# A Fourier-mixing and feed-forward kernel: another written order for some 400 pieces of preparation, and SyncE held to it

## The chip, the cores and the metric

The kernel runs on one core of a Trainium2 chip. The time is the device time of one execution in microseconds (us), lower being better. A core has five engines with queues of their own: TensorE (PE, matrix products; PEld is its loading of weights), VectorE (DVE), ScalarE (ACT), GpSimdE (POOL) and SyncE (SP). An engine works through its own instructions strictly in the order in which the program hands them over; engines wait for one another through semaphores. SP does no arithmetic here: its queue issues transfers between DRAM and on-chip memory, and POOL's queue issues others. A transfer is issued when its queue reaches it and the semaphores it needs have come.

## The reference

```python
h  = x + A(layernorm(x))     # A: a = n @ hid_re.T, b = n @ hid_im.T, y = seq_re @ a - seq_im @ b
h2 = h + B(layernorm(h))     # B: silu(h @ w1) @ w2
```

Here x has 2048 rows of 512 values (f32), the two sequence matrices have 2048 x 2048 values, the two hidden matrices 512 x 512, w1 has 512 x 1792 and w2 1792 x 512. The layer norms have no weights.

## The kernel before

**Products.** Each f32 matrix is split into a rounded part `hi` and a remainder `lo` (`rounded`, L195 on ACT for `hi`, L199 or L201 on DVE for `lo`), and a product is three matrix products, hi by hi, hi by lo and lo by hi (`three`, L245, L246, L247). Much of the arithmetic is in Strassen-like forms: seven products of sums of blocks instead of eight products of blocks, with the sums made by DVE (L647 for the blocks of the sequence matrices), by POOL's accumulating loads (L662), or in the accumulators.

**Stages.** Real part then imaginary part of the sequence matrix on the even rows (`plain`, `fast`), mixing with the hidden matrices (`mix(0)`), the same for the odd rows (`fast` twice and `mix_fast(1)`), then for each half of the rows the layer norm (`norm_h`, with POOL's sum over partitions at L914), the up-projection (`up`), SiLU, and the down-projection (`down`).

**A written order.** The function `program` doesn't run anything itself. It collects about 1500 numbered events. Each has a planned time, and a function that emits a few instructions. `step` adds a block of matrix products at the running planned time of TensorE (0.2265 us for each product) and, at given leads before it, its preparation: loads, roundings, remainders and sums; what reads the accumulators stands at given delays after it. At the end the events are sorted by planned time plus a correction from the table `MOVED`, which names events by their number. `fnet_ffn_kernel` then emits event after event. For the engines in the tuple `ORDERED`, every instruction is tied behind the previous one of the same engine (`issue_after`), so that the engine's queue has exactly the written order. SP isn't in the tuple before: for its transfers the framework's scheduler chooses an order within what data and buffers allow.

**Buffers.** On-chip memory is cut into 51 pages. `Plan.places` hands pages to tiles in the written order, taking the page that is free earliest by plan. So a changed order also changes which page a tile gets, and so whose last use a load has to wait for.

**Names used further on.** `raw` is a 512 KB piece of a sequence matrix as loaded (`load_seq`, L371; the three blocks of a Strassen set by `load`, also L371), `ph` and `pl` are its rounded part and its remainder, `h` is a piece of x for the residual (`load_h`, L737 and L733), `hr`, `m`, `v`, `rs`, `tk` belong to the layer norm, `wal` is the remainder of an up weight, `Ul` and `Vl` are remainders of down weights, `g` is the hidden activation (L1067 to L1073), `vx` an accumulator of the up-projection. The event numbers used below are: 434 to 436, load, rounding and remainder of the imaginary part's block `raw01100`; 439, 443, 447 and 451, the loads of the four blocks `raw01211`, `raw01311`, `raw01011`, `raw01111`; 389 and 391, load of the residual piece `h01` and the sum into it; 475, a sum of blocks with its load 478; 562 and 563, rounding and remainder of `raw11100` for the product 564; 602, a sum of blocks of the last set, with its load 605; 416 and 417, DVE's Newton steps for the layer norm and, at the end of 417, POOL's store `tk`; 657, POOL's accumulating load of `raw11011` for the product 658; 748, the row mean `m10`; 800 and 802, `Ul` and `Vl` of one pair of weights; 890, a `wal`; 861 and 873, additions into `g`; 879 and 882, products of the up-projection.

Of the kernel before, what the change touches and what calls it, by code (L numbers as in the profile page):

```python
# [41 lines left out]
KEEP_US = 2, 0  # L42
FREE_US = {None: 2.0, "matmul": 4.0, "dma_start": 10.0}
MOVED = {
# [42 lines left out]
}  # L87
ORDERED = (mybir.EngineType.PE, mybir.EngineType.DVE, mybir.EngineType.Activation, mybir.EngineType.Pool)


class Stub:
# [44 lines left out]
def fnet_ffn_kernel(  # L136
# [29 lines left out]
    for *_, f in events:  # L166
# [5 lines left out]
        for ins in traced[n:]:  # L172
            if ins.engine in ORDERED:
                last[ins.engine] = ins
# [1199 lines left out]
```

## Time and profile before

| | |
|---|---|
| median of 3 runs | 694.58 us (693.73 to 699.06) |
| profiled execution | 695.98 us, span 694.2 us |
| mean granted TensorE clock | 0.989 |
| PE busy | 674.1 us, 97% of the span, 2916 matrix products |
| DVE busy | 569.2 us, 82% |
| ACT busy | 363.3 us, 52% |
| POOL busy | 99.5 us, 14% |
| transfers | 189.59 MB, mean 273 GB/s |

The span is what the profiler saw between first and last instruction; the time of the same execution is 1.78 us longer. The views quoted in the prediction are these: the page's first line (span), its part 1 (busy time of each engine), part 4 (what the chain that ended last is made of) and parts 5 and 6 (groups of instructions and of transfers); a table by stretches of the span, whose columns are the stretch, its length, then busy time and number of instructions of PE, PEld, DVE, ACT and POOL, the granted clock, the busy share of the 16 DMA engines and GB/s; the list of waits, with total, number and longest in us; and the chain that ended last, in order of time, as start, length and what it was.

### The profile page before, as it was taken

Reading aid. Unit: us, or ns where it says so; the run is one execution under the profiler, and the core shown is the slowest. Engines: PE = TensorE matmul, PEld = TensorE weight load, DVE = VectorE, ACT = ScalarE, POOL = GpSimd, SP = SyncE. Lnnn points to the kernel's source line nnn. Section 1 sums busy time; section 2 is a strip of 40 time slices with the busy share of each in tenths; the row PEclk is TensorE's granted clock in tenths of the full one; section 3 lists DMA queues with packets and bytes.
Section 4 is the critical chain, followed back from the end, with each engine's and each line's share of the span. In section 5 each row is a group of like instructions: output and inputs, shape, how many; then the busy total and the mean of one; then the engine's idle time right before and its main releaser. Section 6 shows DMA issues by size and latency. Waiting matters only on the chain.

```text
span 694.2 us, 8329 instructions
## 1 busy us (share of the span) xinstructions
PE 674.1 (97%) x2916; PEld 550.6 (79%) x2916; DVE 569.2 (82%) x723; ACT 363.3 (52%) x459; POOL 99.5 (14%) x130
## 2 busy tenths in 40 slices
PE   9999999999998899979998998999999999999997
PEld 6888888878886688868886886888888888888886
DVE  7999999898676898789998999766999556549884
ACT  6898656643533443536434654656755444557420
POOL 0011201111221232021411004241100000000000
PEclk9999999999999999999999999999999999999999
DMA  8949989968799976898889998746997496577802
GB/s 317 399 133 286 318 311 334 271 160 320 266 335 397 320 225 152 272 370 292 268 267 306 418 359 291 286 142 193 390 410 304 130 327 228 190 261 249 297 37 92
DMA packets 61786, 189.59 MB, mean 273 GB/s; under 512 B 6960, under 2 KB 14640, under 8 KB 61744
## 3 DMA queue, kind: packets, MB, share of 16 engines
q1 hardware_dynamic: 46608, 136.33, 55.6%
q0 software_dynamic: 14848, 52.46, 23.5%
q8 instruction: 23, 0.38, 0.2%
q10 hardware_dynamic: 288, 0.26, 0.1%
q14 instruction: 19, 0.16, 0.1%
HBM read 142.88 MB, written 46.15 MB: 272 GB/s over the span
## 4 chain that ended last, share of the span: by engine, by line
PE 82%; DVE 7%; DMA 4%; issue 4%; POOL 2%; ACT 1%; DVEq 0%; POOLq 0%; SPq 0%; ACTq 0%
PE m L246 8%; PE m L247 8%; PE m L245 7%; PE y L245 7%; PE y L246 7%; PE y L247 7%; PE f L245 6%; PE f L247 6%; PE f L246 6%; DMA raw<-in_seq 4%; PE c L247 3%; PE c L245 3%; PE c L246 3%; PE vx L245 3%; PE vx L246 3%
## 5 line engine op out<-in xcount | busy, mean ns | idle before, releaser
L195 ACT ACTIVATE ph<-raw 128x1024 fp32r<-128x1024 f32 x102 | 104.7, 1054 | 119.4 <-DMA raw<-in_seq 43.6
L199 DVE TENSOR_TENSOR pl<-raw,ph 128x1024 fp32r<-128x1024 f32 x92 | 110.5, 1219 | 19.4 <-ACT ph L195 18.8
L246 PE MATMUL m<-pl,S 128*128 128x512 f32 x192 | 75.2, 392 | 1.6 <-DVE pl L199 1.6
L245 PE MATMUL m<-ph,S 128*128 128x512 f32 x192 | 75.2, 391 | 0.5 <-ACT ph L195 0.5
L247 PE MATMUL m<-ph,S 128*128 128x512 f32 x192 | 74.7, 389 | 0.0
L1073 DVE TENSOR_TENSOR g<-vx,g 128x512 f32<-128x512 f32 x42 | 28.8, 689 | 48.1 <-PE vx L247 21.4
L246 PE MATMUL m<-pl,X 128*128 128x512 f32 x144 | 58.4, 406 | 6.9 <-DVE pl L199 6.9
L245 PE MATMUL f<-gth,wf 128*128 128x512 f32 x161 | 62.6, 389 | 0.0
L247 PE MATMUL f<-gth,wf 128*128 128x512 f32 x161 | 62.6, 389 | 0.0
L246 PE MATMUL f<-gtl,wf 128*128 128x512 f32 x161 | 62.6, 389 | 0.0
L245 PE MATMUL m<-ph,X 128*128 128x512 f32 x144 | 57.9, 402 | 2.9 <-ACT ph L195 2.9
L195 ACT ACTIVATE gth<-g 128x1024 fp32r<-128x1024 f32 x42 | 42.8, 1052 | 32.2 <-DVE g L1190 29.1
L247 PE MATMUL m<-ph,X 128*128 128x512 f32 x144 | 58.0, 403 | 0.0
L647 DVE TENSOR_TENSOR raw<-raw,raw 128x1024 f32<-128x1024 f32 x36 | 46.6, 1294 | 9.1 <-DMA raw<-in_seq 8.8
L199 DVE TENSOR_TENSOR gtl<-g,gth 128x1024 fp32r<-128x1024 f32 x42 | 50.6, 1215 | 2.9 <-ACT gth L195 2.8
L246 PEld LDWEIGHTS m<-pl,S 128*128 128x128 f32 x192 | 36.3, 189 | 10.7 <-DVE pl L199 3.1
L245 PEld LDWEIGHTS m<-ph,S 128*128 128x128 f32 x192 | 36.3, 189 | 8.5 <-ACT ph L195 0.9
L247 PEld LDWEIGHTS m<-ph,S 128*128 128x128 f32 x192 | 36.1, 188 | 7.3
L246 PEld LDWEIGHTS m<-pl,X 128*128 128x128 f32 x144 | 28.0, 194 | 14.7 <-DVE pl L199 8.8
L1070 ACT ACTIVATE g<-y 128x512 f32<-128x512 f32 x42 | 24.9, 596 | 26.8 <-PE y L247 26.0
L245 PEld LDWEIGHTS m<-ph,X 128*128 128x128 f32 x144 | 27.9, 194 | 9.6 <-ACT ph L195 3.7
L247 PEld LDWEIGHTS f<-gth,wf 128*128 128x128 f32 x161 | 30.2, 188 | 6.3
(334 smaller groups left out, 1588.0 us busy)
## 6 DMA issues: line engine op xcount, KB each, us to landing
raw<-in_seq SPq DMA_DIRECT2D x84, 512.0 KB, 6.9
wf<-wd SPq DMA_DIRECT2D x56, 512.0 KB, 6.2
sf<-sd SPq DMA_DIRECT2D x28, 512.0 KB, 4.9
raw<-in_seq POOLq DMA_DIRECT2D x16, 512.0 KB, 6.4
w<-in_ffn SPq DMA_DIRECT2D x28, 256.0 KB, 4.8
hf<-fd SPq DMA_DIRECT2D x12, 512.0 KB, 7.4
c<-cd SPq DMA_DIRECT2D x8, 512.0 KB, 5.7
h<-in_xT SPq DMA_DIRECT2D x8, 512.0 KB, 9.2
```

The costliest lines, as they stand in the source:

```text
L195: nc.scalar.activation(hi, src, AF.Copy, scale=sign)
L199: nc.vector.tensor_tensor(lo, src, hi, op=ALU.subtract)
L245: nc.tensor.matmul(acc, wh, mh, start=first, stop=False, skip_group_check=on)
L246: nc.tensor.matmul(acc, wh, ml, start=False, stop=False, skip_group_check=on)
L247: nc.tensor.matmul(acc, wl, mh, start=False, stop=last, skip_group_check=on)
L647: nc.vector.tensor_tensor(o, a, b, op=ALU.subtract)
L1070: nc.scalar.activation(g[q, f][:, tau, :], src, AF.Copy)
L1073: nc.vector.tensor_tensor(g[q, f][:, tau, :], src, g[q, f][:, tau, :], op=ALU.add)
```

## The change

Two things change. The table `MOVED` gets other entries, some 400 in each version, so that many loads, roundings, remainders, sums and stores stand earlier or later in the written order. TensorE's blocks stay in the same order. And SP joins `ORDERED`, so its transfers are issued in the written order as well. No instruction is added or removed on any engine: PE has 2916 matrix products, ACT 459 instructions, SP 305 transfers in both.

```diff
 MOVED = {
-    0: -36.389, 1: -26.974, 2: -25.939, 4: -11.243, 5: -2.693, 6: -13.747, 12: 14.791, 14: 14.711, 16: 18.149,
...
-    382: -6.701, 385: -6.084, 386: 12.11, 389: -8.794, 392: 29.565, 393: 10.825, 394: -2.4, 395: -5.773, 396: -8.195,
-    399: 0.585, 407: 9.82, 413: 3.675, 416: 9.909, 417: 10.994, 418: 18.286, 419: 14.954, 420: 19.968, 421: 22.38,
-    426: -13.409, 427: -12.306, 428: -9.978, 431: -5.315, 434: -7.091, 435: -8.466, 448: 5.682, 449: 6.113,
-    457: 5.344, 458: 6.173, 466: 3.109, 470: 3.472, 472: 4.448, 473: 2.565, 474: 3.664, 475: 4.827, 476: 3.713,
...
-    562: 7.247, 563: 6.96, 566: -21.988, 567: -8.316, 568: -8.975, 571: -7.565, 572: -2.707, 583: -10.317,
-    584: -9.857, 585: -10.429, 591: -8.989, 600: -9.323, 602: -14.47, 603: -9.883, 604: -9.605, 605: -13.05,
...
-    652: -17.791, 655: 6.183, 656: 6.402, 657: 8.938, 660: 3.784, 666: 3.041, 667: 5.105, 668: 2.916, 669: 9.103,
...
-    743: -16.636, 744: -15.219, 747: 8.561, 748: 5.353, 749: 1.425, 750: 8.476, 751: 5.341, 752: 5.487, 753: 5.039,
...
-    791: -29.354, 793: 21.242, 796: 17.891, 797: 18.541, 798: 15.638, 799: 30.528, 800: 30.551, 801: 22.376,
-    802: 28.878, 803: 30.882, 804: -37.203, 805: -35.339, 806: -22.187, 807: -16.326, 810: 6.765, 811: -11.914,
...
-    849: 10.95, 850: -35.58, 851: -12.549, 852: -12.388, 853: -12.17, 861: 6.54, 862: 5.955, 864: 2.581, 865: 5.264,
-    871: 1.743, 873: 2.177, 874: 4.867, 876: 2.03, 881: 14.176, 890: 0.614, 922: -0.032, 923: -1.532, 1040: 3.011,
...
+    0: -28.65, 28: 5.71, 32: 7.37, 35: 4.85, 36: 5.08, 38: 5.92, 39: 3.77, 40: 11.88, 41: 4.45, 42: 5.82, 46: 6.79,
...
+    371: -2.93, 379: 15.77, 380: -5.83, 381: -9.58, 382: -11.55, 383: -10.71, 385: -12.74, 389: 15.56, 392: 31.21,
...
+    413: 2.52, 416: 2.35, 419: 4.93, 421: 4.41, 422: -5.38, 423: -11.72, 424: -12.78, 427: 1.2, 434: -20.43,
+    435: 8.14, 436: 7.8, 441: 6.79, 444: 6.24, 445: 7.12, 448: 6.88, 449: 4.71, 456: 6.48, 457: 6.32, 458: 4.15,
+    469: 3.35, 470: 4.72, 475: -7.82, 478: -8.29, 480: -9.25, 481: -3.04, 486: 5.35, 487: 3.91, 490: 6.07, 493: 3.56,
...
+    551: -22.18, 562: -1.92, 566: -13.21, 567: -7.28, 572: 4.19, 575: 2.87, 576: 4.05, 578: 8.24, 579: 2.78,
+    580: 2.84, 582: 12.19, 583: -11.4, 584: -6.49, 585: -8.06, 591: -11.48, 597: 5.63, 600: -8.75, 602: -6.54,
+    603: -5.42, 604: -6.58, 605: -7.77, 615: -5.2, 616: -5.83, 618: -10.76, 628: 5.64, 632: -4.62, 635: -9.76,
...
+    739: 5.09, 740: -12.75, 741: -12.8, 743: -5.88, 748: 10.99, 749: 12.27, 750: 14.31, 751: 14.39, 752: 15.61,
...
+    793: 19.36, 794: -6.35, 795: -1.97, 796: 16.67, 797: -43.41, 799: 25.35, 800: 23.26, 801: 12.21, 802: 23.15,
...
 }
-ORDERED = (mybir.EngineType.PE, mybir.EngineType.DVE, mybir.EngineType.Activation, mybir.EngineType.Pool)
+ORDERED = (
+    mybir.EngineType.PE, mybir.EngineType.DVE, mybir.EngineType.Activation, mybir.EngineType.Pool, mybir.EngineType.SP,
+)
```

Of the events named above, 436 and 478 have no entry before; 417, 563, 657, 861, 873 and 890 have none after.

63 rows, old and new, of the table MOVED are left out of this document.

## The prediction

> **What bounds the kernel now.** I read the page's first parts first, to see which engine could set the time.
>
> ```profile
> span 694.2 us, 8329 instructions
> PE 674.1 (97%) x2916; PEld 550.6 (79%) x2916; DVE 569.2 (82%) x723; ACT 363.3 (52%) x459; POOL 99.5 (14%) x130
> PE 82%; DVE 7%; DMA 4%; issue 4%; POOL 2%; ACT 1%; DVEq 0%; POOLq 0%; SPq 0%; ACTq 0%
> ```
>
> TensorE is busy for 97% and makes 82% of the chain that ended last; the rest of the chain is what TensorE waited for. No matrix product is taken away, so the change can only win or lose waits. Next, where they lie: the table by stretches, PE busy being its second number.
>
> ```profile
> 216.00:244.00 28.00, 23.31 (x92) 17.62 (x91) 21.37 (x22) 11.69 (x14) 4.95 (x3) 0.94 0.95 341
> 300.00:314.00 14.00, 9.95 (x37) 7.71 (x36) 11.17 (x9) 4.18 (x6) 4.93 (x3) 0.88 0.94 369
> 360.00:376.00 16.00, 13.73 (x53) 10.62 (x52) 12.49 (x16) 6.87 (x8) 2.01 (x3) 0.89 0.94 265
> 428.00:442.00 14.00, 11.23 (x43) 8.78 (x43) 13.36 (x15) 6.48 (x11) 8.17 (x8) 0.88 0.79 296
> 437.50:690.00 252.50, 252.47 (x1113) 208.47 (x1111) 185.18 (x245) 129.15 (x179) 16.33 (x20) 1.00 0.68 240
> 26.00:100.00 74.00, 73.98 (x327) 60.95 (x326) 71.42 (x110) 55.48 (x73) 11.34 (x17) 1.00 0.88 284
> ```
>
> In the undisturbed 252.50 us one product takes 252.50/1113 = 0.227 us. The four short stretches need (92-1), (37-1), (53-1) and (43-1) times 0.227, one product being cut by a border; they lose 7.3, 5.8, 4.2 and 4.5 us, together **21.8 us**. Part of each loss is not waiting but a granted clock of 0.88 to 0.94. Everything else is nearly full: after 437 TensorE loses 0.03. So the least that a better order could give is about 695.98 - 21.8 = 674 for the profiled execution.
>
> What ended these waits is in the chain, in order of time.
>
> ```profile
> 214.93 8.05 DMA raw<-in_seq
> 223.06 1.07 ACT ph L195
> ...
> 225.29 1.22 DVE pl L199
> ...
> 236.44 1.24 DVE pl L199
> 237.72 0.50 PE m L246
> 239.15 0.42 PE m L245
> 239.56 0.43 PE m L246
> ...
> 294.37 9.36 DMA raw<-in_seq
> 303.91 1.05 issue
> 304.96 1.23 DVE pl L199
> 306.23 0.50 PE m L246
> ...
> 313.66 1.22 DVE pl L199
> 314.88 1.14 DVE raw L647
> ...
> 356.24 0.53 POOL tk L955
> 356.77 8.62 DMA raw<-in_seq
> 365.47 1.06 ACT ph L195
> 366.56 1.24 DVE pl L199
> 367.84 0.50 PE m L246
> ...
> 421.59 1.13 DVE Ul L199
> ...
> 430.37 1.14 DVE m L912
> 431.57 0.57 issue
> 432.14 1.29 DVE g L1073 x2
> 433.48 0.72 PE vx L245
> ```
>
> Three waits begin with a transfer of a sequence block (`raw<-in_seq`), the fourth with DVE's own queue.
>
> **The change part by part.** All counts stay, so no duration is added; each part moves what an engine does next.
>
> First wait, 216 to 244 (7.3 us). Events 439, 443 and 447 are written well ahead of 214.93, but before the change SP's order has 451 in front of them, whose page was held by a store from `hS10l`.
>
> ```profile
> SPq L371 <- DMA fd<-hS10l: 8.3, 1, 8.3
> h<-in_xT SPq DMA_DIRECT2D x8, 512.0 KB, 9.2
> ```
>
> In the written order 439 and 443 stand ahead of 451 and are spared up to those 8.3 us. What is late next: the remainder 436 now stands behind the sum 391, whose load 389 moves behind 443. That load needs the page of an earlier `pl`, about 207 by DVE's new order, and lands 9.2 later, 216; then 1.2 for the sum, 1.07 and 1.22 for the pair `ph`, `pl` (whose page is free only after another store, about 218): TensorE, which wants it at 218, waits some 2.4. The sum 475 now stands in front of two remainders on DVE and waits for its load 478, about 217 plus 8: another 2.3. I keep 5.3 of the 7.3 with what the clock adds, so **2.0 goes**; bounds 7.3 and -3 (475's load later by its own 2 to 3 us).
>
> Here the Trainium skill bears on what a leftover costs. After 237.72 the products start 0.43 apart, half speed, for some 3.4 us, 1.7 lost. "TensorE: Matmul & The Clock Gate", part 1, says the clock is cut by an activity window of about 3.4 us; split waits would then cost no half-speed spell, and 2.0 would become 3.7. The half speed here followed several waits in one stretch, so the row doesn't decide, and the sum goes without it.
>
> Second wait, 300 to 314 (5.8). DVE stood at the sum 602 for the load issued at 294.37 and landed at 303.73, while the `pl` for product 564 stood behind it. Now 563 stands ahead of 602 and seven other pieces, so this wait goes. What is late next: DVE's remainders for the following products, which already make up the chain again from 313.66 (`pl`, then `raw`). I keep half: **3.0 goes**, bounds 0 and 5.8.
>
> Third wait, 360 to 376 (4.2). On POOL's queue the accumulating load 657 stands behind the store `tk`, which waited for DVE's Newton steps till 356.24. They are moved ahead of some five pieces of 1.1 to 1.2 us, about 7 us earlier; load, `ph` and `pl` then end near 361, and the product wants them at 363.6. **4.2 goes**; bounds 0 and 4.2.
>
> Fourth wait, 428 to 442 (4.5). Here DVE is late by its own work.
>
> ```profile
> 372.00:430.00 58.00, 58.00 (x257) 48.06 (x256) 55.66 (x53) 29.99 (x33) 9.94 (x13) 1.00 0.93 349
> DVE raw L647 <- DMA raw<-in_seq: 4.1, 2, 2.7
> DVE pl L199 <- ACT ph L195: 4.5, 3, 3.5
> ```
>
> It works 55.66 of 58 us, so whatever TensorE gains earlier, it arrives here and finds DVE no further. Ahead of product 882 (2.7 us of TensorE behind 879) DVE's new queue holds two weight remainders of 1.13 more (`Ul`, `Vl`) and the mean's two pieces less, from 430.37 to the additions at 432.14, 1.8: some 0.5 net. So DVE allows 882 earlier by 2.7 - 0.5 = **2.2 plus what DVE itself is earlier**. DVE is earlier where it stood in the same waits as TensorE: 2.0 in the first and 3.0 in the second (it waited 4.1 and 4.5 there and behind for loads and roundings), 5.0 together; bounds 0 and 8.6 + 2.0. In the third it did other work. So the gain at 437 is 5.0 + 2.2 = **7.2**, although TensorE alone would have 2.0 + 3.0 + 4.2 = 9.2 by then.
>
> The start, 26 to 100. DVE works 71.42 of 74 us, and sums and weight pieces are pulled forward into it; up to some 2 us of remainders come late at 80 to 130. SP's order also puts two loads behind five others; their `ph` are moved later too, so nothing stands for them. Near 283 a remainder stands behind three other DVE pieces of about 1.2 and may be 2.7 late. I count all of these at nothing, because DVE's work up to 437 is the sum and a wait of TensorE in between is cover that it had anyway; if DVE isn't late at 433, they cost up to 4.7.
>
> After 437 DVE has 67 us to spare, and TensorE waits nowhere; some 100 stores and loads move there. Nothing, with a bound of 5.8 for one wait like the second.
>
> Sum: 695.98 - 7.2 = 688.8 for the profiled execution, which is 1.40 above the median of the runs; against the median 694.58 - 7.2 = 687.4. I predict **687**.
>
> **The rivals.**
>
> *All four waits go.* If DVE's standing for loads (8.6 in the second half, 2.0 and more in the first) goes too, 16 to 21 us are won: 674 to 679. For it: all three causes upstream are reordered. Against it: DVE's 55.66 of 58 us. Chance 0.20.
>
> *The waits only move.* DVE gains nothing upstream, and one new wait near 283 (2.7) and one after 437 eat the 2.2: 690 to 698. For it: 436 and 475 are put behind late loads. Chance 0.12.
>
> *The loads land no earlier.* The DMA engines are busy 0.94 to 0.95 of the first and second wait; a load issued 8 us earlier then shares the engines with those that went before, and lands as it did. The first wait's 2.0 and DVE's part of the second, 3.0, are gone: 694.58 - 2.2 = 692.4. The Trainium skill, "DMA: Bandwidth & Descriptors", section "Issuing engines are not separate DMA queues", says that transfers run on the same 16 engines whoever issues them, and that issuing only saves time on the sequencer; by that rule this would be the time. Against it: outside the waits the share is 0.68 to 0.93, so there is room. Chance 0.06.
>
> *SyncE blocks (the slower side).* Held to an order, SP stands at a load whose page isn't free, and every load behind it stands too, also those whose page is free.
>
> ```profile
> SPq L371 <- PE m L247: 47.5, 14, 13.4
> raw<-in_seq SPq DMA_DIRECT2D x84, 512.0 KB, 6.9
> ```
>
> Before, SP could stand 13.4 us without harm, since the scheduler put loads that nobody needed behind it. A stand of 13.4 ahead of a load with 6.9 to land takes 20.3, against the 18 us by which loads are written ahead: 2.3 late, and 1.7 for the half clock, 4.0 each. It decides from the third such place on, beyond the 7.2 won: five of them are 20.0 - 7.2, 707. The places would be 185 to 225, where h loads are now in the row, and 385 to 410. Chance 0.18.
>
> *The change doesn't do what it says:* the pages held, not the order, set when SP issues, and the table's shifts cancel. Then 694.6. Chance 0.02.
>
> **How the numbers follow.** The forecast has 0.42, with 681 to 692 as its own range, since the first wait may lose 5.3 more than taken and the second 2.8, against some 5 the other way. A measurement of this kernel tells about 1% (6.9 us) from no change; the borders are 687.6 and 701.5. Faster by over 1%: 0.20 from all four waits and 0.25 from the forecast, whose unknowns reach further down than up: 0.45. Slower by over 1%: 0.18 from SyncE and 0.02 from waits that move and add up: 0.20. Within 1%: the remaining 0.35, namely 0.17 of the forecast, 0.10 of the moved waits, 0.06 of late landing and 0.02 of no effect. The range is 676 to 704: below it lies about half of the first rival (0.10), above it about half of the blocking case (0.10).
>
> **What would show it.** In the changed profile the wait at 306 and the one that starts at `tk` near 356 should be gone from TensorE's waits; SP's 8.3 us for the store of `hS10l` should stand behind the loads 439 and 443; a wait for `pl` of two to three us should remain at 216 to 230; and TensorE's longest wait should be on DVE near 425 to 435. The prediction is wrong if DVE reaches 433 more than 8 us earlier, if `raw<-in_seq` takes over 9 us to land where issues are earlier, or if a new SP stand shows in TensorE's chain, before 200 or after 440.

## The result

The changed kernel takes 686.09 us in the median of 6 runs (683.38 to 688.73); the kernel before, beside it, 695.25 (692.62 to 699.06). The ratio is 0.9867 with a 95% interval of 0.9826 to 0.9908: 9.2 us or 1.3% less. The forecast was 687, faster by 1.1%, with 676 to 704 as the range. The profiled execution took 684.59 us, 11.4 less than that of before.

The page of the changed kernel, its first line and part 1:

```profile
span 682.8 us, 8329 instructions
PE 668.7 (98%) x2916; PEld 546.2 (80%) x2916; DVE 573.2 (84%) x723; ACT 363.7 (53%) x459; POOL 98.0 (14%) x130
```

The counts are those of before, and DVE works 4.0 us more, not less. What went is waiting. The table by stretches of the changed kernel, PE busy with its number of products first, answers to the four stretches of the prediction (later parts lie up to 12 us earlier now):

```profile
216.00:234.00 18.00, 14.46 (x55) 10.99 (x54) 11.00 (x11) 7.99 (x9) 4.60 (x5) 0.91 0.91 371
300.00:314.00 14.00, 14.00 (x64) 11.58 (x63) 13.96 (x13) 6.43 (x8) 4.91 (x3) 1.00 1.00 400
345.00:361.00 16.00, 16.00 (x72) 13.20 (x72) 15.97 (x19) 8.00 (x10) 4.62 (x8) 1.00 1.04 332
418.00:432.00 14.00, 13.21 (x58) 10.28 (x57) 13.97 (x17) 8.62 (x13) 7.42 (x10) 1.00 0.94 354
```

At 0.227 us each, (55-1) products take 12.3 of the first 18.00: 5.7 is lost there still, of 7.3. The second and third are full. The fourth loses 1.1 of 4.5. What is left is in TensorE's waits:

```profile
PE m L250 <- DVE pl L203: 4.9, 4, 2.8
PE c L249 <- ACT C L500: 1.1, 1, 1.1
PE vx L250 <- DVE T4l L203: 0.7, 1, 0.7
```

Before, the first of these rows was 8.5 with a longest wait of 4.1. For the experiments I use one measure throughout: where two products start more than 0.06 us further apart than 0.227, the excess is a loss, half speed included. Summed by place, in us of each profiled execution (places are given as in the kernel before; single profiles differ at one place by 2 to 3 us where loads decide; the first 10 us, with 2.0 to 3.1 in each kernel, are left out):

| kernel | to 198 | 200-290 | near 306 | near 366 | near 433 | later | all |
|---|---|---|---|---|---|---|---|
| before | 1.8 | 7.6 | 5.9 | 4.4 | 4.6 | 0.3 | 24.7 |
| changed | 2.4 | 6.5 | 1.1 | 0.4 | 1.3 | 1.2 | 13.0 |
| sp_only | 2.4 | 10.2 | 1.9 | 6.2 | 4.6 | 0.3 | 25.6 |
| table_only | 4.8 | 8.2 | 1.1 | 0.4 | 1.3 | 2.5 | 18.5 |
| two_waits | 1.4 | 8.8 | 0.2 | 7.9 | 5.9 | 0.3 | 24.5 |
| three_waits | 1.1 | 8.9 | 0.7 | 3.5 | 6.4 | 0.3 | 20.9 |
| mean_late | 2.8 | 7.4 | 6.8 | 1.7 | 3.4 | 0.4 | 22.5 |
| four_moves | 2.3 | 8.3 | 0.8 | 2.6 | 4.9 | 0.4 | 19.3 |
| four_moves_sp | 1.9 | 10.2 | 0.0 | 0.5 | 4.8 | 0.4 | 17.8 |
| mean_back | 4.6 | 9.2 | 1.1 | 0.4 | 7.1 | 1.8 | 24.3 |
| stores_first | 3.7 | 9.0 | 0.9 | 0.4 | 1.3 | 0.9 | 16.3 |
| sum_later | 5.0 | 7.6 | 1.1 | 0.4 | 1.3 | 1.0 | 16.4 |
| stores_and_sum | 5.7 | 5.7 | 0.9 | 0.4 | 1.3 | 1.1 | 15.1 |
| three_sums | 1.6 | 4.3 | 0.9 | 0.4 | 1.3 | 2.2 | 10.7 |

The loss fell by 11.7 us, against 11.4 between the two profiled executions. The three places near 306, 366 and 433 went from 14.9 to 2.8, 12.1 less (4.8, 4.0 and 3.3); the stretch at 200 to 290 gave 1.1; and 0.6 + 0.9 = 1.5 were given back before 198 and later. Part of it is the clock: spells of some 3.4 us in which the products start 0.43 apart, each losing 1.7, come four times in the kernel before (from 239, 307, 369 and 434) and once in the changed one (from 229). That is some 5 of the 11.7.

### The profile page after: what moved, and what is told of

Read it like the earlier page. It is cut to its first block, busy times and chain, and to the rows that moved or that the text cites. A ratio compares the mean times of both kernels' runs of the same rounds, so it can differ in the third digit from the quotient of the medians.

```text
span 682.8 us, 8329 instructions
## 1 busy us (share of the span) xinstructions
PE 668.7 (98%) x2916; PEld 546.2 (80%) x2916; DVE 573.2 (84%) x723; ACT 363.7 (53%) x459; POOL 98.0 (14%) x130
## 4 chain that ended last, share of the span: by engine, by line
PE 46%; DVE 9%; issue 7%; DMA 3%; POOL 2%; ACT 0%; DVEq 0%; POOLq 0%
PE m L250 5%; PE m L251 5%; PE m L249 5%; PE f L250 5%; PE f L251 5%; PE f L249 5%; PE y L251 4%; PE y L250 4%; PE y L249 4%; DVE pl L203 2%; DVE gtl L203 2%; PE vx L251 1%; PE vx L249 1%; PE vx L250 1%; DVE g L1194 1%
## 5 line engine op out<-in xcount | busy, mean ns | idle before, releaser
L203 DVE TENSOR_TENSOR pl<-raw,ph 128x1024 fp32r<-128x1024 f32 x92 | 114.3, 1263 | 18.9 <-ACT ph L199 14.1
L250 PE MATMUL m<-pl,X 128*128 128x512 f32 x144 | 56.3, 391 | 1.6 <-DVE pl L203 1.6
L249 PE MATMUL m<-ph,X 128*128 128x512 f32 x144 | 56.1, 390 | 0.0
L251 PE MATMUL m<-ph,X 128*128 128x512 f32 x144 | 56.0, 389 | 0.0
L249 PEld LDWEIGHTS f<-gth,wf 128*128 128x128 f32 x161 | 30.2, 188 | 7.0 <-ACT p L1213 0.7
L250 PEld LDWEIGHTS f<-gtl,wf 128*128 128x128 f32 x161 | 30.2, 188 | 7.0 <-DVE gtl L203 0.7
L251 PEld LDWEIGHTS f<-gth,wf 128*128 128x128 f32 x161 | 30.2, 188 | 6.3
## 6 DMA issues: line engine op xcount, KB each, us to landing
hf<-fd SPq DMA_DIRECT2D x12, 512.0 KB, 10.7
```

The source lines that it names most:

```text
L203: nc.vector.tensor_tensor(lo, src, hi, op=ALU.subtract)
L249: nc.tensor.matmul(acc, wh, mh, start=first, stop=False, skip_group_check=on)
L250: nc.tensor.matmul(acc, wh, ml, start=False, stop=False, skip_group_check=on)
L251: nc.tensor.matmul(acc, wl, mh, start=False, stop=last, skip_group_check=on)
```

## The experiments

**Which half of the change does it.** First the order of SyncE alone, then the table alone.

```diff
 # sp_only: the old table
-ORDERED = (mybir.EngineType.PE, mybir.EngineType.DVE, mybir.EngineType.Activation, mybir.EngineType.Pool)
+ORDERED = (mybir.EngineType.PE, mybir.EngineType.DVE, mybir.EngineType.Activation, mybir.EngineType.Pool, mybir.EngineType.SP)
```

> The kernel before with SyncE held to the written order and the old table. Theory (the table removes the waits at 306, 356 and 433; the order of SyncE alone frees the loads 439 and 443 from the store of hS10l): the first wait shrinks by 3 to 6 us of its 7.3, the other three stay, and DVE at 433 lets only part of it through: 690 to 693. Rival (the order of SyncE alone is the whole gain): about 686. Rival (a fixed order blocks SyncE at pages that the old table did not foresee): over 698.

Measured: 697.04 us, ratio to before 1.0021 (0.9998 to 1.0044). No gain; the expected 690 to 693 was missed, and the blocking rival's "over 698" wasn't reached either. The waits near 306 and 366 together went from 10.3 to 8.1, but the stretch at 200 to 290 lost 2.6 more. In this kernel's list of SyncE's waits from 194 to 211, its transfers and DVE's queue, SyncE blocks in the way the slower rival described:

```profile
SPq L371 <- DVE pl L199: 8.5, 1, 8.5
```

```profile
194.35 14.37 SPq L371 DMA_DIRECT2D raw<-in_seq  x4
208.82 0.91 SPq L737 DMA_DIRECT2D h<-in_xT  x2
```

```profile
214.59 1.23 DVE L743 TENSOR_TENSOR h<-y,h 128x1024 f32<-128x1024 f32 x1 [6.22 <-DMA h<-in_xT]
```

SyncE stood 8.5 us at a block's page, the residual's load behind it was issued at 208.82 only, and DVE stood 6.2 us for it. TensorE stood from 210 to 216 and ran at half speed till 219, 7.3 us lost. So the mechanism is real; with the changed table the h loads stand elsewhere, and table_only, next, shows no cost of it.

```diff
 # table_only: the new table, SyncE left to the scheduler
-    mybir.EngineType.PE, mybir.EngineType.DVE, mybir.EngineType.Activation, mybir.EngineType.Pool, mybir.EngineType.SP,
+    mybir.EngineType.PE, mybir.EngineType.DVE, mybir.EngineType.Activation, mybir.EngineType.Pool,
```

> The changed kernel with its table but SyncE left to the scheduler's order. Theory: the waits at 306, 356 and 433 stay away, because they are set by the queues of DVE and POOL; only loads shift: 685 to 689, within 3 us of the changed kernel's 686.1. Rival (the table needs SyncE's order): 692 or more, with new waits of TensorE on loads.

Measured: 687.49 us, ratio 0.9887 (0.9857 to 0.9916), the changed kernel's being 0.9867 (0.9826 to 0.9908). The intervals lie over each other. The three late waits are gone exactly as in the changed kernel (1.1, 0.4, 1.3). The two profiles differ by 5.5 us of loss, mostly before 290 and after 447, where loads decide; the medians don't separate the kernels. So the table makes the gain, and SyncE's order adds nothing that these runs can tell.

**Whether the late waits are worth their length.** The kernel before, with the moves that the prediction held responsible for the second and third wait.

```diff
 # two_waits
-    416: 9.909, 417: 10.994, 602: -14.47,
+    416: 2.35, 602: -6.54,
```

> The kernel before with two moves alone: the sum 602 behind the remainder 563, and DVE's Newton steps 416 and 417 (with POOL's store tk) earlier. Theory as in the prediction (DVE decides at 433): the waits at 306 and 356, 10.0 us together, mostly go, but DVE arrives at 433 only 3 to 5 us earlier, the wait there grows from 4.5 to 8 or more, and the time falls by 3 to 5: 690 to 692. Rival (each wait is worth its own length): the time falls by 9 to 10, 685 to 686, and the wait at 433 stays at 4 to 5.

Measured: 694.23 us, ratio 0.9976 (0.9954 to 0.9998). (In this kernel the sum 602 also falls behind the sum 603, which overwrites one of its inputs, so it takes the difference from other values; the work is the same.) The wait near 306 went from 5.9 to 0.2. The one near 366 did not go: 7.9. The expected 690 to 692 was missed. The chain shows a second cause:

```profile
356.62 5.77 DMA u<-in_ffn
362.52 0.42 DVE v L1133
362.94 0.34 DVE v L1134
363.28 0.35 DVE v L1135
363.99 2.37 DVE pl L199 x2
```

```profile
DVE v L1133 <- DMA u<-in_ffn: 2.1, 1, 2.1
```

DVE stood 2.1 us, from 360.4, at the first sum of the down weights (791) till its load, issued at 356.62, had landed, and the remainder for product 658 was behind it and behind the four sums, 1.5 us of work. With `tk` late this was hidden. The changed table also moves 790 and 791, and it writes the load 657 itself 8.9 us earlier.

```diff
 # three_waits
-    416: 9.909, 417: 10.994, 602: -14.47, 790: -20.48, 791: -29.354,
+    416: 2.35, 602: -10.5, 790: -23.55, 791: -16.22,
```

> The kernel before with the sum 602 just behind the remainder 563, the Newton steps 416 and 417 with the store tk earlier, and in addition the down weights' load 790 and its DVE sums 791 at the places of the changed table, since with the first two moves alone DVE stood at that sum from about 348 till its load, issued at 356.6, had landed at 362.4, and the remainder for product 658 stood behind it. Theory: 306 and 366 lose less than 2 us together instead of 10.0; DVE at 433 lets part of it through, its wait grows from 4.5 to 7 or more: 690 to 692. Rival (each wait is worth its own length): 686 to 687 and the wait at 433 stays 4 to 5. If the wait near 366 is still there, the cause found is not the last one.

Measured: 692.40 us, ratio 0.9953 (0.9935 to 0.9971). Near 306 and 366 the loss fell from 10.3 to 4.2, and near 433 it rose from 4.6 to 6.4: 6.1 won upstream gave 3.3 us in the end. The expected 690 to 692 was missed by little; 1.9 of what was left came from a new wait at 347. DVE lets only a part through: 1.8 of the 6.1 came back near 433, and another 1.3 at 200 to 290, where loads decide. (The expectation says that in two_waits DVE stood from about 348; its queue was busy up to 360.4, and it stood 2.1.)

**What sets the wait near 433.** The row mean moved alone, in the kernel before and back in the changed one.

```diff
 # mean_late (kernel before)
-    748: 5.353,
+    748: 8.653,
```

> The kernel before with the row mean m10 (event 748) behind the two additions into g that product 879 needs, and nothing else. Theory (DVE's queue sets the wait at 433): the additions come 1.8 us earlier, TensorE's wait there falls from 4.5 to about 2.7, the time by about 2: 693. Rival (the load or ACT sets it): no change. What the changed kernel won there would then be due to the other moves.

Measured: 694.23 us, ratio 0.9985 (0.9968 to 1.0001). The loss went from 4.6 to 3.4: the wait at 430 is 1.2 now, and 2.2 turned up at 441 to 445, at products further down. By itself the move wins 1 us or nothing, less than the 2 expected.

The mean isn't all that stood there. Product 879 writes the accumulator tile that the addition 861 reads, and 882 that of 873. Before, the additions into `g` are written in the order 864, 873, 861, and 879 starts when the last of them ends:

```profile
429.69 0.68 DVE L1073 TENSOR_TENSOR g<-vx,g 128x512 f32<-128x512 f32 x1
432.14 1.28 DVE L1073 TENSOR_TENSOR g<-vx,g 128x512 f32<-128x512 f32 x2
433.48 0.72 PE L245 MATMUL vx<-T4h,wah 128*128 128x512 f32 x1 [2.77 <-DVE g L1073]
```

The changed table writes 861 first, then 864, and 873 last, as the addition at 423.11:

```profile
414.71 0.69 DVE L1077 TENSOR_TENSOR g<-vx,g 128x512 f32<-128x512 f32 x1
418.16 0.68 DVE L1077 TENSOR_TENSOR g<-vx,g 128x512 f32<-128x512 f32 x1
421.25 0.39 PE L249 MATMUL vx<-T4h,wah 128*128 128x512 f32 x1
423.85 0.50 PE L249 MATMUL vx<-T7h,sf 128*128 128x512 f32 x1
```

So 861 is out of the way 18.0 us earlier, 879 (the row at 421.25) waits for no addition any more, and 873 holds 882 only, whose first product is the last row. No run moves the additions alone; what that is worth by itself isn't shown.

```diff
 # four_moves (kernel before)
-    416: 9.909, 417: 10.994, 602: -14.47, 748: 5.353, 790: -20.48, 791: -29.354,
+    416: 2.35, 602: -10.5, 748: 8.653, 790: -23.55, 791: -16.22,
# four_moves_sp: and
+ORDERED = (mybir.EngineType.PE, mybir.EngineType.DVE, mybir.EngineType.Activation, mybir.EngineType.Pool, mybir.EngineType.SP)
```

> The moves of three_waits and of mean_late together, SyncE left to the scheduler. Theory (three waits upstream stop at DVE near 430, so the mean's place is worth more with them than alone): the wait near 430, 5.4 us in three_waits, falls by 2 to 4 and the time to 688.5 to 690.5. Rival (independent parts): 692.4 less 2 is 690.4, the wait falls by no more than in mean_late.

> As four_moves, with SyncE held to the written order of this table. Theory (the order of SyncE is worth nothing by itself, its loads stand where the pages come free): within 2 us of four_moves. Rival (with the late waits gone SyncE's order counts): 3 us or more below it.

Measured: 691.05 us, ratio 0.9934 (0.9910 to 0.9959), and 690.26 us, ratio 0.9929 (0.9905 to 0.9953). The four named moves give half of the change, and they add up about as independent parts (0.9953 and 0.9985 give 0.9938), as the rival had it and not the theory. Again SyncE's order makes no difference, also with the late waits mostly gone. The remaining 0.6% to the changed kernel comes from moves that I didn't take singly, the additions among them.

```diff
 # mean_back (changed kernel)
-    748: 10.99,
+    748: 3.0,
```

> The changed kernel with the row mean m10 (event 748, two DVE pieces of 1.8 us) back in front of the remainder T4l and the addition into g that product 879 needs. Theory (DVE decides at 422, as in the prediction's fourth wait): TensorE's wait there, 1.3 us, becomes 3 to 4.5 with the half clock, the time rises by about 2: 688. Rival (DVE has slack there now): no change, 686.

Measured: 693.47 us, ratio 0.9968 (0.9950 to 0.9986), some 7 us more than the changed kernel for 1.8 us of work that is moved. In the profiles it loses 11.3 more: 5.8 near 433, where the loss went from 1.3 to 7.1, three times the estimate, and 4.9 before 290, where loads decide. DVE's queue and POOL's in mean_back:

```profile
425.89 1.21 DVE L916 TENSOR_TENSOR m<-h,h 128x1024 f32<-128x1024 f32 x1
427.13 0.69 DVE L917 TENSOR_TENSOR m<-m 128x512 f32<-128x512 f32 x1
427.74 1.22 DVE L203 TENSOR_TENSOR T4l<-hn,T4h 128x1024 fp32r<-128x1024 f32 x1
428.88 3.00 DVE L342 TENSOR_TENSOR wal<-w,wah 128x768 fp32r<-128x768 f32 x1
431.80 0.68 DVE L1077 TENSOR_TENSOR g<-vx,g 128x512 f32<-128x512 f32 x1
```

```profile
427.92 4.13 POOL L918 PARTITION_ALL_REDUCE m<-m  x1 [2.91 <-DVE m L917]
```

And the same two pieces in the changed kernel:

```profile
421.10 1.23 DVE L203 TENSOR_TENSOR T4l<-hn,T4h 128x1024 fp32r<-128x1024 f32 x1
422.25 0.95 DVE L342 TENSOR_TENSOR wal<-w,wah 128x768 fp32r<-128x768 f32 x1
```

The mean brings POOL's sum over partitions with it. It ends at 432.05, and the `wal` that started beside it takes 3.00 instead of 0.95. So the move is worth 1.85 to `T4l` and another 2.05 to the addition, and the half clock that followed the longer wait made it 5.8. TensorE stands at both, at 879 for `T4l` and at 882 for the addition 873 (the expectation put that addition at 879):

```profile
429.02 0.50 PE L250 MATMUL vx<-T4l,wah 128*128 128x512 f32 x1 [2.53 <-DVE T4l L203]
432.53 0.80 PE L249 MATMUL vx<-T7h,sf 128*128 128x512 f32 x1 [1.71 <-DVE g L1077]
```

**What is left at 216 to 233.** The chain of the changed kernel ends its largest remaining wait with a store, and POOL's queue shows when that was issued.

```profile
219.02 6.67 DMA fd<-hS11l
225.69 2.06 issue
227.75 1.24 DVE pl L203
```

```profile
215.35 3.24 POOL L918 PARTITION_ALL_REDUCE m<-m  x1 [9.17 <-DVE m L917]
218.47 0.56 POOL L772 DMA_DIRECT2D fd<-hS11h  x1
219.02 0.53 POOL L772 DMA_DIRECT2D fd<-hS11l  x1
```

```diff
 # stores_first: +    386: -2.5,
 # sum_later:    -    475: -7.82,   +    475: -2.0,
 # stores_and_sum: both
```

> The changed kernel with the two stores of hS11 (event 386) ahead of the row mean's sum over partitions on POOL. In the changed kernel TensorE's largest wait that is left, 4.7 us at 229 to 233, ends with the landing of such a store, issued at 219.0 behind that sum (3.24 us). Theory: the stores go out about 7 us earlier, the wait falls to 0 to 1.5, and since DVE at 422 is only 1.3 late, 2 to 4 us come through: 682 to 684. Rival (DVE decides at 422): the wait at 422 grows by what was won, 686.

> The changed kernel with the sum 475 behind the three remainders 453, 445 and 449 instead of in front. Theory (the wait at 229 to 233 is ended by the store of hS11l, which holds the page of the remainder 445): the wait stays at 4 to 5 us, 686. Rival (DVE stands at the sum for its load, as the prediction had it): the wait falls by 2 or more, 683 to 684.

> The changed kernel with both: the two stores of hS11 ahead of the sum over partitions, and the sum 475 behind the three remainders. With the stores alone DVE stood 5.9 us at that sum for a load that took 13.7 us to land. Theory (the two causes stand one behind the other): the wait at 229 to 233 falls from 4.7 to under 2, and 682 to 684 comes out. Rival (the stores slow the loads, so some other remainder is late): the wait stays above 3 and the time at 686 or more.

Measured: 689.58 us, ratio 0.9921 (0.9895 to 0.9948); 687.00 us, ratio 0.9867 (0.9844 to 0.9891); 685.41 us, ratio 0.9855 (0.9834 to 0.9876). Alone, neither move helps: the loss in this stretch was 9.0 and 7.6, against 6.5 in the changed kernel. That fits the theory for sum_later and speaks against it for stores_first. Together it is 5.7, and the piece at 229 to 233 fell to 0.2 as expected, though the time didn't reach the expected 682 to 684. With the stores first, the chain has the sum 475 waiting for its load:

```profile
215.48 13.73 DMA raw<-in_seq
...
229.77 0.70 issue
230.47 2.36 DVE pl L203 x2
```

With the sum later, DVE's queue names the store itself:

```profile
231.71 2.36 DVE L203 TENSOR_TENSOR pl<-raw,ph 128x1024 fp32r<-128x1024 f32 x2 [5.55 <-DMA fd<-hS11l]
```

Two causes stood one behind the other here too. The time doesn't separate stores_and_sum from the changed kernel, since its profile lost 4.5 at 123 to 128, where DVE stood 3.9 us at another sum for its load. That sum can be put back as well.

```diff
 # three_sums: stores_and_sum and
-    273: 0.53,
+    273: 5.0,
```

> stores_and_sum with one more piece behind what needs nothing from it: the sum 273, which stood on DVE for its load (3.9 us there, 1.2 in the changed kernel) ahead of the remainder 259 that product 264 needs, now stands behind 259. Theory: the wait at 123 to 128 (4.5 us in stores_and_sum, 0.9 to 3.8 in other profiles of the changed table) falls under 1.5; the time to 682 to 684. Rival (DVE is full there, so another remainder is late by as much): 685 to 686.

Measured: 682.64 us, ratio 0.9830 (0.9802 to 0.9857), the best of all. The table by stretches of this kernel:

```profile
216.00:242.00 26.00, 23.98 (x104) 18.81 (x103) 19.59 (x19) 14.09 (x17) 1.97 (x4) 1.00 0.76 303
118.00:130.00 12.00, 12.00 (x54) 9.89 (x53) 11.88 (x11) 7.26 (x9) 2.25 (x4) 1.00 1.04 374
```

The wait at 123 is gone, and the time is in the expected 682 to 684. The intervals of three_sums, stores_and_sum (0.9834 to 0.9876) and the changed kernel (0.9826 to 0.9908) still lie partly over each other, so the times alone don't show how much of this is won.

## Why the prediction was right, and where it wasn't

**The sum.** 7.2 us were forecast, 9.2 came out in the medians and 11.4 between the profiled executions. The direction, the bound (waits of TensorE that DVE lets through in part) and, by the medians, the size within a third were right; "faster by over 1%" was the likeliest outcome named, with 0.45. The sum hangs on DVE, and that term was too small. That 687 lies within 1 us of 686.09 is partly luck: 5.1 us too little up to product 882 stands against 0.9 lost later, and against profiled executions that lie further apart than the medians.

**DVE's part, the mis-sized term.** The prediction let DVE be 5.0 us earlier at the fourth wait. The table by stretches up to the addition into `g` where the two meet (the end of 861 before, the start of 873 after), in the kernel before and then in the changed one, DVE busy being the fourth number:

```profile
0.00:433.40 433.40, 417.62 (x1794) 339.01 (x1794) 379.52 (x475) 230.48 (x275) 79.69 (x108) 0.99 0.87 295
```

```profile
0.00:423.10 423.10, 413.85 (x1798) 336.83 (x1799) 379.74 (x473) 231.31 (x277) 79.71 (x111) 1.00 0.87 299
```

The same amount of work, but DVE idles 433.40 - 379.52 = 53.9 before and 43.4 after: 10.5 us less. This is a balance and says where time went, not who held whom. Cut where DVE has done 256.7 us of work, it shows the place:

```profile
300.00:433.40 133.40, 124.38 (x531) 101.40 (x529) 122.78 (x133) 66.17 (x73) 29.37 (x32) 0.97 0.91 320
```

```profile
298.10:423.10 125.00, 123.26 (x541) 101.08 (x540) 123.07 (x131) 65.77 (x74) 29.61 (x35) 1.00 0.93 332
```

Behind the cut DVE idled 10.6 before and 1.9 after, 8.7 less; ahead of it 1.8 less. So the 2.0 for the first wait was right, and the 3.0 for the second half was the step that failed: it should have been nearly all of the 8.6 that the prediction itself read there (4.1 for loads, 4.5 for roundings) and used as its bound only. After, 0.9 is left of them:

```profile
DVE pl L203 <- ACT ph L199: 0.9, 2, 0.6
```

Two things went wrong. Half of the second wait was kept for what might be late next, and DVE stood for nothing there. And "In the third it did other work" was misread: the longest of those stands lies there.

```profile
366.56 2.36 DVE L199 TENSOR_TENSOR pl<-raw,ph 128x1024 fp32r<-128x1024 f32 x2 [3.47 <-ACT ph L195]
```

Not every wait of DVE that goes is won. Near 190 a wait went at which TensorE lost nothing, and in the changed kernel another stands in its place (the first row is of before):

```profile
DVE ws L1014 <- DMA fd<-hS01l: 5.2, 1, 5.2
```

```profile
DVE pl L203 <- ACT ph L199: 5.0, 1, 5.0
```

The view that gives the term is DVE's whole idle time ahead of the point, stretch by stretch, not the waits at TensorE's.

**First wait.** 2.0 of 7.3 was to go; 1.6 went, 1.1 over the whole stretch of the table. The size was right. Of the two causes, the first is there, smaller (1.1 at 219 to 221, behind a stand of DVE of 1.2 for an `h` load); the second wasn't: in the changed kernel the wait at 229 is the store of `hS11l` behind POOL's sum over partitions (sum_later leaves it), not the sum 475. That one is the next in line (stores_first brings it out). The leftover did bring half speed: behind one wait of 2.8 the products start 0.43 apart from 229.4 to 232.4, 1.7 us of the 5.7. Splitting a wait doesn't always avoid it: in table_only such a spell, from 124 to 128, follows two waits of 1.0 each.

**Second wait.** 3.0 of 5.8 was to go; all of it went, and the remainders at 313 weren't late: 1.1 turned up at 324. I had halved it for what DVE was doing next, although DVE had just been let off 2.7 us of standing there.

**Third wait.** 4.2 forecast and gone. Its cause was only half found: two_waits shows that `tk` alone leaves it, because the sums 791 and their load stood in front of the remainder.

**Fourth wait.** It was to grow, since TensorE would come earlier than DVE; it shrank from 4.6 to 1.3, because TensorE came 9.3 us earlier, as forecast (9.2, though by another split: 0.5 up to 290, 4.8 near 306 and 4.0 near 366; the last product ahead of 879 starts at 421.02 instead of 430.32), but DVE allowed 12.3 instead of 7.2. That the wait grows when TensorE wins more than DVE holds in three_waits, where it went to 6.4. That 882 and no longer 879 is held by an addition was right, and so was the form of the sum: 2.7 us between 879 and 882 (at the half speed of the kernel before; 1.4 at full speed), less 0.9 of further work ahead of the addition (0.5 in the prediction; POOL's sum slowing `Ul` by 1.4 is part of it), and 10.5 less idle time make 12.3. Product 882 starts at 423.85 instead of 436.13, 12.3 earlier. mean_back isn't the price of the mean's move, as it puts the mean ahead of `T4l`, further ahead than the kernel before had it; mean_late is, with 1.2.

**Counted at nothing.** The start was priced at nothing because DVE would be late at 433 anyway. DVE's own stands count there too: against stores_and_sum, three_sums loses 4.1 less up to 198 (5.7 and 1.6), where DVE had stood 3.9 us for a load, and the profiled execution is 4.3 shorter (1.7 by the ratios to before, whose intervals lie partly over each other). After 437, 0.9 us came in, so "nothing" was nearly right.

**The signs named.** TensorE's waits at 306 and from `tk` are gone as said, SyncE no longer stands for the store of `hS10l`, and 2.8 us for a `pl` remain at 229. Two signs came out against me: TensorE's longest wait is this one and not one on DVE near 430, and DVE has the same work behind it 10.3 us earlier (423.10 and 433.40), where more than 8 was to count as wrong. The place of the last wait and DVE's term were wrong, then. The loads of the sequence blocks take 6.9 us to land in the median, as before; I didn't follow the earlier ones singly.

**The rivals.** All four waits did nearly go, as the first rival had it, but for the one at 216 to 233. SyncE blocks with the old table (sp_only); with the new one table_only shows no cost of its order. That loads land no earlier has one case: in stores_first, with the DMA engines at a busy share of 1.03 from 215 to 229, a load took 13.7 us against a median of 6.8, and that cost what was won there; the first wait's remainder in the changed kernel hangs on a store instead. That only the waits move is what two_waits did. What stays open is which of the other moves make the last 0.6%, the additions' above all, and whether SyncE's order is worth some 2 us or nothing.

## What to carry to other kernels

Where a second engine is nearly as full as the first, count all of its idle time ahead of the point where the two meet, stretch by stretch, and what may take its place; a wait of its own that goes is time won there only if no other comes in. Look also at which piece the first engine meets: here the order of three additions changed which product was held. A wait named in the chain often hides the next: before a move is priced, look for what else stands in the same queue ahead of the piece that is needed, and price the last of them. In a strictly ordered queue a piece that waits for a load belongs behind all that doesn't need it.

## What the runs showed of the hardware

DVE's pieces slow down beside POOL's sum over partitions. In mean_back `wal` took 3.00 instead of 0.95, to within 0.2 us of the sum's end. POOL's sum takes 3.23 us where it began first (414.93 in the changed kernel); it took 4.13 in mean_back, where DVE's `T4l` had begun 0.18 before it and ran 1.04 beyond its start. The Trainium skill, "SBUF — State Buffer", section "Who interferes with whom", says that a DVE instruction with two inputs in SBUF contends with a GpSimd instruction that reads SBUF, through one shared pair of ports that is an exclusive lock, and that the order of issue decides who blocks. Both numbers agree with it: the later one paid, each time. In the changed kernel the sum and the piece beside it:

```profile
414.93 3.23 POOL L918 PARTITION_ALL_REDUCE m<-m  x1 [3.21 <-PE vx L251]
```

```profile
415.60 2.65 DVE L203 TENSOR_TENSOR Ul<-u,Uh 128x1024 fp32r<-128x1024 f32 x1 [0.19 <-ACT Uh L199]
```

The `Ul` there takes 2.65 instead of 1.21 and ends with the sum, at 418.2; the chain leads from it to `T4l`, for which product 879 waits. The two measured cases cost DVE 2.05 and 1.44 us. The busy times of DVE hide this cost, as the blocked time counts as busy.
